# Layer 1 of a linear-attention and MLP kernel: a row of ones in the key weights, and the keys' feature map in one VectorE operation

## The chip, the cores and the metric

The kernel runs on one core of one Trainium2 chip. The metric is the device time of one execution in microseconds (us). The kernel before was run three times: 760.4, 760.68 and 760.71 us, median 760.68 us. One further execution was recorded by the hardware profiler; its span, from the first to the last instruction, is 758.4 us.

The engines are called as the profile calls them: PE (TensorE matmuls), PEld (TensorE weight loads), DVE (VectorE), ACT (ScalarE), POOL (GpSimd), SP (SyncE, which issues the transfers here).

## The reference, cut to what matters

A linear attention block A and an MLP block B alternate twice over 2048 tokens of width 576. Everything below concerns the feature map `phi` of the first block A.

```python
def _A_ref(x, wqkv, wo):                       # x: (1, 2048, 576), already layer-normed
    H = 32; Dh = D // H                        # 32 heads of 18
    q, k, v = split(x @ wqkv)
    phi = lambda t: jnp.where(t > 0, t + 1, jnp.exp(t)) + 1e-6
    pq, pk = phi(q), phi(k)
    kv = jnp.einsum("bhsd,bhse->bhde", pk, v)
    z = jnp.einsum("bhsd->bhd", pk)
    num = jnp.einsum("bhqd,bhde->bhqe", pq, kv)
    den = jnp.einsum("bhqd,bhd->bhq", pq, z)[..., None] + 1e-6
    return (num / den).reshape(B, S, D) @ wo

x = x + _A_ref(_layernorm(x), A_wqkv, A_wo)    # layer 1: li = 0 in the kernel
x = x + _B_ref(_layernorm(x), ...)             # li = 1
x = x + _A_ref(_layernorm(x), A_wqkv, A_wo)    # li = 2
x = x + _B_ref(_layernorm(x), ...)             # li = 3
```

## The kernel before, in words

The 2048 tokens are 16 row tiles of 128 (`NT`). For PE the normed rows are also needed turned: `yT` holds them as five chunks of 128 features (576 is 4.5 chunks, and the lower half of chunk 4 meets zero weights). In layer 1 a row tile is loaded (L188), its mean and variance are taken on DVE (L397, L398, L404), it is normed in place (L444 on POOL, L449 on DVE for tiles 0 to 3), PE transposes its five blocks (L500, out `tp`) and ACT copies them into `yT` (L505; tiles 0 and 1 are split between ACT L502 and DVE L503). Normed columns 512 to 575 do not stay in the row: a second norm instruction writes them to `v_ring`, beside a column of ones put there at the start (L222, L223). These 65 columns are called the tail.

The attention never forms V per token. For each half of the 576 key columns (288, `HALF`) and each row tile, `k_half` (L650) makes the keys in PSUM, `phi` turns them into `pk`, and `rows_by_keys` (L668) adds normed rows times `pk` into four accumulators (`acc`, 128 rows each) and a fifth for the tail (65 rows, the 65th being the sum of `pk` over tokens, `z`). In the loop over row tiles only half 0 is summed. Half 1 is kept and summed after the loop (`last_rows_by_keys`, `sums`).

Two forms of `phi` stand in layer 1 before the change:

- half 0 (`phi_from_psum`, L547; tile 2 excepted): ACT exp (L554), ACT adds 1 + 1e-6 (L555), then DVE takes min and adds 1e-6 (L560) and takes the max of two bf16 tiles in SBUF (L562). PSUM is last read by ACT.
- half 1 (`phi_by_dve`, L535): ACT exp (L537), DVE min and add (L539), DVE adds to the PSUM operand and takes the max (L541). PSUM is last read by DVE.

PSUM has eight banks. Four belong to the two pairs `accA` and `accB`; four (`ps_h`, L41) go round among everything else. From the start of the tail sums to the end of the loop the tail's accumulator (L673) holds one of these four, so keys of half 0 (`k_ps`), keys of half 1 (`k_ps`), the transposes (`tp`) and one query product (`q_ps`, L621) of each row tile go round in three.

The order of PE is the program's order, since every matmul is chained to the one before (`pe`, L166). In the loop of layer 1 (L860 to L868, t = 4 to 15) it is, for each t: keys half 0, keys half 1 (5 matmuls each), five transposes of a later row tile, one query product (5 matmuls of 512 columns), then the sums of row tile t (the tail first, then four). The queues of the other engines are ordered by the tile framework, except where the program adds an order: the beginning is written out by hand for DVE and ACT in two lists (`in_order`, L854 to L856; names such as `n0` norm, `nt0` norm of the tail, `s0a` statistics, `e00` exp, `id00` add, `mi00` min, `ma00` max, tile and half), later statistics stand behind the last max of the keys, and `yT` copies stand behind the last exp of the keys. The queue of SP is chained for the loads.

In layer 3 (li = 2) the normed rows come back through DRAM: `load_row` loads columns 0 to 511 (L293) and a separate transfer per four row tiles loads the tails (L333). One query product per row tile stands there too, but no transposes: rows are turned by DVE and transfers.

Of the kernel before, what the change touches and what calls it, by code (L numbers as in the profile page):

```python
# [15 lines left out]
P = 128  # L16
# [14 lines left out]
HALF = D // 2  # L31
LAST_PARTS = (slice(0, 3 * P), slice(3 * P, D))
# [3 lines left out]
def build(tc, A_x, A_wqkv, A_wo, B_w1, B_b1, B_w2, B_b2, out, dbg=None, n_layers=4):  # L36
    nc = tc.nc
    dbg = dbg or {}
    with ExitStack() as ctx:
# [95 lines left out]
        NV = 2  # L135
        v_ring = [const.tile([P, G, P], BF16, name=f"v_ring{i}") for i in range(NV)]
# [10 lines left out]
        def row_tile(name):  # L147
            return rows.tile([P, D], F32, name=name, tag="row")

        x0_tiles = {}  # L150

# [32 lines left out]
        def load_x0(t):  # L184
            if t % 2 == 0:
                x0_tiles["pair"] = rows.tile([P, 2, D], BF16, name="x0", tag="row")
            x0 = x0_tiles["pair"][:, t % 2, :]
            chained(nc.sync.dma_start(out=x0, in_=x_in[t * P:(t + 1) * P, :]))  # L188
            x0_tiles[t] = x0
# [31 lines left out]
        for vr in v_ring:  # L221
            nc.gpsimd.memset(vr[:], 0.0)  # L222
            nc.gpsimd.memset(vr[:].rearrange("p g c -> p (g c)")[:, 0:520].rearrange("p (t e) -> p t e", e=65)[:, :, 64:65], 1.0)  # L223
# [42 lines left out]
        def tail_of(t):  # L266

            flat = v_ring[t // 8][:].rearrange("p g c -> p (g c)")
            return flat[:, (t % 8) * 65:(t % 8 + 1) * 65]

        def tails(c):
            flat = v_ring[c // 2][:].rearrange("p g c -> p (g c)")
            return flat[:, (c % 2) * 260:(c % 2 + 1) * 260].rearrange("p (t e) -> p t e", e=65)

        def first_tail(t, width=65):

            slot = 2 * (t % 8) + t // 8
            flat = v_ring[slot // 8][:].rearrange("p g c -> p (g c)")
            return flat[:, (slot % 8) * 65:(slot % 8) * 65 + width]

# [8 lines left out]
        def load_row(t):  # L289
            if t % 2 == 0:  # L290
                pair = rows.tile([P, 2, D], BF16, name="yrow_pair", tag="row")
                row_of[t], row_of[t + 1] = pair[:, 0, :], pair[:, 1, :]
            load = nc.sync.dma_start(out=row_of[t][:, 0:4 * P], in_=yrow_d[t // TPC, t % TPC].rearrange("j r d -> (j r) d")[:, 0:4 * P])  # L293
            if t >= 6:
                behind(load, "landed")
# [20 lines left out]
        def land(now=False):  # L316

            for it in list(landing):
                it[0] -= 1
                if it[0] > 0 and not now:  # L320
                    continue
                _, home, c, kind = it
                landing.remove(it)
                cols = slice(c * CB, (c + 1) * CB)
                nc.sync.dma_start(out=yT[:, 0:KD - 1, cols],
                                  in_=home[0:16, :, :].rearrange("(k jj) r n -> (jj r) k n", jj=4))
                for hi in range(2 if kind == "B" else 1):
                    landed = nc.sync.dma_start(out=yT[64 * hi:64 * (hi + 1), KD - 1, cols],
                                      in_=home[16:18, :, :].rearrange("jj r n -> (jj r) n"))
                if kind == "A":  # L330
                    if c == NCB - 1:
                        sp_last["landed"] = landed.ins.name
                    tail = nc.sync.dma_start(out=tails(c)[:, :, 0:64],  # L333
                                             in_=yrow_d[c].rearrange("i j r d -> (j r) i d")[:, :, 4 * P:D])
                    behind(tail, "landed")
                    if c == NCB - 1:
                        for t in range(c * TPC, NT):
                            load_row(t)
# [8 lines left out]
        class LNPipe:  # L347
# [11 lines left out]
            def tick(self, transposes=1):  # L359
                land()  # L360
                for it in list(self.items):
# [77 lines left out]
                    elif st in (2, 3) and it["kind"] == "A" and it["evac"] == "act":  # L439
                        xt, t = it["xt"], it["t"]  # L440
                        tail = first_tail(t)[:, 0:64]
                        if it["norm"] == "pool":
                            for out, cols in ((xt[:, 0:4 * P], slice(0, 4 * P)), (tail, slice(4 * P, D))):
                                norm = nc.gpsimd.tensor_scalar(out=out, in0=xt[:, cols], scalar1=it["rstd"][:, 0:1],  # L444
                                                               scalar2=it["nmr"][:, 0:1], op0=ALU.mult, op1=ALU.add)
                            pool_last["norm"] = norm.ins.name
                        else:
                            for name, out, cols in ((f"n{t}", xt[:, 0:4 * P], slice(0, 4 * P)), (f"nt{t}", tail, slice(4 * P, D))):
                                norm = named(name, nc.vector.tensor_scalar(  # L449
                                    out=out, in0=xt[:, cols], scalar1=it["mv"][:, 0:1], scalar2=it["rstd"][:, 0:1],  # L450
                                    op0=ALU.subtract, op1=ALU.mult))
                            dve_last["norm"] = norm.ins.name
# [30 lines left out]
                    elif st == 4:  # L483
# [14 lines left out]
                        for k in range(KD):  # L498
                            block = first_tail(t, P) if first_layer and k == 4 else y[:, k * P:(k + 1) * P]
                            pe(nc.tensor.transpose(out=(tp if k < 3 else tp2)[:, k, :], in_=block, identity=ident[:]))  # L500
# [34 lines left out]
        def phi_by_dve(ps_ap, out_ap, rows, n, tag=None):  # L535
            e = exp_tile(tag)
            exp = nc.scalar.activation(out=e[0:rows, 0:n], in_=ps_ap, func=ACT.Exp)  # L537
            act_last["exp"] = exp.ins.name
            low = nc.vector.tensor_scalar(out=e[0:rows, 0:n], in0=e[0:rows, 0:n], scalar1=1.0, scalar2=1e-6,  # L539
                                          op0=ALU.min, op1=ALU.add)  # L540
            top = nc.vector.scalar_tensor_tensor(out=out_ap, in0=ps_ap, scalar=C1, in1=e[0:rows, 0:n],  # L541
                                                 op0=ALU.add, op1=ALU.max)
            dve_last["phi"] = top.ins.name
            if tag is not None:
                named("e" + tag, exp), named("mi" + tag, low), named("ma" + tag, top)

# [68 lines left out]
        def layer_A(li, next_kind, pre_a1=None):  # L615
# [34 lines left out]
            def k_half(t, half, defer=False):  # L650
# [5 lines left out]
                by_dve = half or li == 0 and t == 2  # L656

                def phi():
                    if (half, t // 2) not in self_k["pk"]:
                        self_k["pk"][(half, t // 2)] = blk.tile([P, D], BF16, name="pk", tag="blk")  # L660
                    pk = self_k["pk"][(half, t // 2)][:, (t % 2) * HALF:(t % 2 + 1) * HALF]
                    (phi_by_dve if by_dve else phi_from_psum)(kp[:, 0:HALF], pk, P, HALF,
                                                              tag=f"{t}{half}" if li == 0 and t < 4 else None)
                if defer:
                    return phi
                phi()

            def rows_by_keys(t, half, chunks=(4, 0, 1, 2, 3), done=True):  # L668
# [5 lines left out]
                pk = self_k["pk"][(half, t // 2)][:, (t % 2) * HALF:(t % 2 + 1) * HALF]  # L674
                for k in chunks:
                    dst = self_k["tail"][0:65, 0:HALF] if k == 4 else self_k["acc"][k // 2][:, k % 2, 0:HALF]
                    lhsT = (tail_of(t) if li > 0 else first_tail(t)) if k == 4 else row_of[t][:, k * P:(k + 1) * P]
                    pe(nc.tensor.matmul(dst, lhsT=lhsT, rhs=pk, start=(t == 0), stop=(t == NT - 1)))  # L678
                cols = slice(half * HALF, (half + 1) * HALF)
                if 4 in chunks and t == NT - 1:  # L680
                    nc.gpsimd.memset(zk[:, cols], 0.0)
                    nc.scalar.copy(out=k2[4][0:64, cols], in_=self_k["tail"][0:64, 0:HALF])
                    nc.scalar.copy(out=zk[64:65, cols], in_=self_k["tail"][64:65, 0:HALF])
                if not done:
                    return
                if t % 2:
# [7 lines left out]
                for i, copy in enumerate((nc.scalar.copy, nc.vector.tensor_copy)):  # L694
                    for j in range(2):
                        copy(out=k2[2 * i + j][:, cols], in_=self_k["acc"][i][:, j, 0:HALF])

            def last_rows_by_keys():

                parts = [ps_h.tile([P, 512], F32, name=name, tag="h") for name in ("z_rows", "k2_tail")]  # L700
                for size, part in zip((32, 64), parts):
                    n = P // size
                    for t in range(NT):
                        tail = tail_of(t) if li > 0 else first_tail(t)
                        lhsT = tail[:, 64:65].to_broadcast([P, 32]) if size == 32 else tail[:, 0:64]
# [3 lines left out]
                nc.scalar.activation(out=zk[:, HALF:D], in_=parts[0][:, 0:HALF], func=ACT.Identity, scale=1.0 / 32)  # L709
                nc.scalar.copy(out=k2[4][:, HALF:D], in_=parts[1][:, 0:HALF])  # L710
# [36 lines left out]
            def z_stage():  # L747
                zp = ps_h.tile([P, 512], F32, name="z_ps", tag="h")
                for g in range(G):
                    pe(nc.tensor.matmul(zp[0:GR[g], g:g + 1], lhsT=zk[:, GO[g]:GO[g] + GR[g]],  # L750
                                        rhs=(tail_of(0) if li > 0 else first_tail(0))[:, 64:65],
# [73 lines left out]
            if li == 0:  # L825
# [3 lines left out]

                def feed_and_tick(t, n):  # L830
                    feed0(t, after=dve_last["phi"] if t > 5 else None)
                    for _ in range(n):
# [21 lines left out]
                in_order("s0a s0b g0 s1a s1b n0 nt0 g1 cd0 n1 nt1 s2a s2b g2 cd1 mi00 s3a n2 nt2 s3b ma00 g3 u3 mi10 s4a "  # L854
                         "mi11 n3 ma10 nt3 ma11 mi20 ma20 mi21 s4b ma21 g4 u4 mi01 ma01 s5a s5b mi30 g5 mi31 u5 ma30 ma31")
                in_order("ln0 re0 ln1 re1 ca0 e00 ca1 ln2 re2 id00 e01 e10 ca2 e11 id10 e20 e21 ca3 e31 e30 id30 ca4")  # L856
# [292 lines left out]
        for li, kind in enumerate(kinds):  # L1149
# [11 lines left out]
            else:  # L1161
                pe_chain.update(on=True)
# [50 lines left out]
```

## Time and profile before

| | before |
|---|---|
| runs, us | 760.4, 760.68, 760.71 |
| median, us | 760.68 |
| profiled execution, span, us | 758.4 |
| PE busy | 753.2 us, 99% |
| ACT busy | 328.7 us, 43% |
| DVE busy | 272.0 us, 36% |
| POOL busy | 116.6 us, 15% |
| granted TensorE clock | 1.000 |
| layer 1 to its first MLP matmul | 0 to 101.8 us |

The profiled execution is told by its span; the 2.3 us between the span and the median of the runs lie around it. A timeline line reads: start, length, engine, line, operation, output <- input, size; in brackets the idle time of the engine just before and what ended it. The chain of work that ended last reads: start, length, engine and what it ran; it names at each moment the one piece of work that the end waited for. A group line reads: line, engine, operation, names, shapes, count | busy us, mean ns | idle before.

### The profile page before, as it was taken

The numbers are of one execution on the slowest core, as the hardware profiler recorded it, in microseconds if no ns is written. First come the engines' busy times: TensorE is split into PE (matmuls) and PEld (weight loads), VectorE is DVE, ScalarE is ACT, GpSimd is POOL, SyncE is SP. The second block draws the span as 40 slices with busy tenths as digits, with TensorE's granted clock in tenths as the row PEclk, the third lists the DMA queues.
The fourth block names the chain that finished last, engine by engine and source line by source line (L and its number), as shares of the span: only waits on it lengthen the run. The fifth ranks groups of instructions, "written<-read, shape, count | busy, mean of one in ns | idle before, by whom it ended". The sixth has DMA issues, their size and how long they took to land.

```text
span 758.4 us, 15817 instructions
## 1 busy us (share of the span) xinstructions
PE 753.2 (99%) x6595; PEld 487.4 (64%) x6595; DVE 272.0 (36%) x685; ACT 328.7 (43%) x733; POOL 116.6 (15%) x196
## 2 busy tenths in 40 slices
PE   9999999999999999999999999999999999999998
PEld 5776754774477457646777777457646754774476
DVE  8876862136033503401367577600230131000000
ACT  6887656205600650263057666660174036205600
POOL 4840231002000301200100005300020020001000
PEclk9999999999999999999999999999999999999999
DMA  8994573026312711320404047530240033011000
GB/s 236 267 313 74 178 262 82 17 64 189 83 39 83 181 51 48 109 69 17 131 24 116 24 136 255 185 82 16 88 115 7 16 127 82 9 33 55 1 9 24
DMA packets 80977, 73.90 MB, mean 97 GB/s; under 512 B 36874, under 2 KB 65546, under 8 KB 80906
## 3 DMA queue, kind: packets, MB, share of 16 engines
q1 hardware_dynamic: 80906, 72.90, 33.0%
q8 instruction: 51, 0.84, 0.5%
q14 instruction: 20, 0.16, 0.1%
HBM read 48.10 MB, written 24.77 MB: 96 GB/s over the span
## 4 chain that ended last, share of the span: by engine, by line
PE 97%; DVE 1%; ACT 0%; issue 0%; DVEq 0%
PE m_ps L1104 36%; PE h_ps L1045 21%; PE hp_ps L1045 16%; PE q_ps L621 6%; PE k_ps L653 5%; PE wo_ps L933 5%; PE k_ps L678 4%; PE m_half L1104 1%; PE tp L500 1%; PE warm_ps L217 1%; PE k_tail L678 1%; PE kv_ps L719 0%; PE den_ps L769 0%; PE rden_ps L810 0%; PE kvwo_half L737 0%
## 5 line engine op out<-in xcount | busy, mean ns | idle before, releaser
L1104 PE MATMUL m_ps<-w_sb,hT 128*128 128x288 bf16 x2232 | 274.8, 286 | 0.0
L1104 PEld LDWEIGHTS <-hT 128*128 128x128 bf16 x2304 | 224.3, 98 | 60.4 <-issue 3.4
L1045 PEld LDWEIGHTS <-w_sb 64*128 64x128 bf16 x2304 | 124.5, 94 | 136.4 <-issue 1.9
L1045 PE MATMUL hp_ps<-yT,w_sb 64*128 64x512 bf16 x1152 | 178.0, 376 | 0.0
L1045 PE MATMUL h_ps<-yT,w_sb 64*128 64x512 bf16 x1152 | 148.0, 376 | 0.0
L1050 ACT COPY relay_sb<-relay_sb 128x1 f32<-128x1 f32 x144 | 28.5, 198 | 260.4 <-PE h_ps L1045 217.6
L1041 ACT ACTIVATE hT<-h_ps,b1T 128x512 bf16<-128x512 f32 x144 | 91.0, 683 | 44.1 <-PE h_ps L1045 44.1
L433 POOL TENSOR_TENSOR ln_rstd<-ln_u,neg_half 128x1 f32<-128x1 f32 x61 | 35.2, 577 | 439.9 <-DVE ln_u L415 218.0
L1041 ACT ACTIVATE hT<-hp_ps,b1T 128x512 bf16<-128x512 f32 x144 | 91.1, 692 | 0.0
L605 DVE TENSOR_TENSOR xbf<-m_ps,xo 128x576 bf16<-128x576 f32 x15 | 11.4, 757 | 213.5 <-PE m_ps L1104 213.5
L605 DVE TENSOR_TENSOR xo<-m_ps,xo 128x576 f32<-128x576 f32 x16 | 12.1, 757 | 172.6 <-PE m_ps L1104 172.6
L588 POOL TENSOR_TENSOR xo<-xo,b_bc 128x576 f32<-128x576 f32 x32 | 40.9, 1283 | 97.3 <-DMA xo<-x_d 58.4
L1045 PE MATMUL h_ps<-yT,w_tail 64*128 64x512 bf16 x144 | 54.1, 376 | 0.0
L1045 PE MATMUL hp_ps<-yT,w_tail 64*128 64x512 bf16 x144 | 54.1, 376 | 0.0
L621 PE MATMUL q_ps<-yT,wqkv_sb 128*126 128x512 bf16 (+1 forms) x200 | 49.3, 379 | 0.1
L653 PE MATMUL k_ps<-wqkv_sb,yT 128*128 128x288 bf16 x320 | 44.6, 286 | 0.2
L933 PE MATMUL wo_ps<-kvwo,pq 126*128 126x288 bf16 (+1 forms) x320 | 43.4, 286 | 0.3
L1045 PEld LDWEIGHTS <-w_tail 64*128 64x128 bf16 x288 | 27.1, 94 | 17.1
L653 PEld LDWEIGHTS <-yT 128*128 128x128 bf16 x320 | 31.0, 98 | 8.9 <-ACT yT L502 0.6
L933 PEld LDWEIGHTS <-pq 126*128 126x128 bf16 (+1 forms) x320 | 30.3, 97 | 9.1 <-issue 0.8
L621 PEld LDWEIGHTS <-wqkv_sb 128*126 128x126 bf16 (+1 forms) x200 | 25.7, 131 | 11.7 <-issue 0.5
L554 ACT ACTIVATE phi_e<-q_ps 126x512 bf16<-126x512 f32 (+1 forms) x40 | 23.9, 597 | 18.4 <-PE q_ps L621 16.8
(138 smaller groups left out, 591.6 us busy)
## 6 DMA issues: line engine op xcount, KB each, us to landing
xo<-x_d SPq DMA_DIRECT2D x48, 288.0 KB, 3.5
x_d<-xo SPq DMA_DIRECT2D x32, 288.0 KB, 2.6
xl<-x_d SPq DMA_DIRECT2D x24, 288.0 KB, 4.2
y_d<-turned SPq DMA_DIRECT2D x40, 144.0 KB, 3.1
w_sb<-in_B_w_dram SPq DMA_DIRECT2D x6, 864.0 KB, 10.4
yT<-y_d SPq DMA_DIRECT2D x10, 512.0 KB, 4.2
w_sb<-in_B_w_dram SPq DMA_DIRECT2D x9, 512.0 KB, 5.9
x_d<-xn SPq DMA_DIRECT2D x16, 288.0 KB, 3.3
```

The costliest lines, as they stand in the source:

```text
L433: nc.gpsimd.tensor_tensor(out=rstd[:], in0=it["u"][:], in1=neg_half[:], op=ALU.pow)
L554: exp = nc.scalar.activation(out=e_out, in_=ps_ap, func=ACT.Exp)
L588: nc.gpsimd.tensor_tensor(out=xo[:], in0=xo[:], in1=b2_bc[:], op=ALU.add)
L605: total = nc.vector.tensor_tensor(out=xn[:, cols].rearrange("p (h n) -> p h n", h=2), in0=halves, in1=xo[:, cols].rearrange("p (h n) -> p ...
L621: pe(nc.tensor.matmul(qp[0:GR[g], :], lhsT=wqkv_sb[:, k, GO[g]:GO[g] + GR[g]], rhs=yT[:, k, c * CA:(c + 1) * CA], start=(k == 0), stop=(k ...
L653: pe(nc.tensor.matmul(kp[:, 0:HALF], lhsT=yT[:, k, t * P:(t + 1) * P], rhs=wqkv_sb[:, k, D + half * HALF: D + (half + 1) * HALF], start=(k ...
L678: pe(nc.tensor.matmul(dst, lhsT=lhsT, rhs=pk, start=(t == 0), stop=(t == NT - 1)))
L933: pe(nc.tensor.matmul(wp[:, half, 0:HALF], lhsT=pq[(g, c)][0:GR[g], j * P:(j + 1) * P], rhs=kvwo[g][0:GR[g], half * HALF:(half + 1) * HALF ...
L1041: act_last["gelu"] = nc.scalar.activation(out=to, in_=ps, func=ACT.Gelu_apprx_tanh, bias=b1T[:, f:f + 1], scale=1.0).ins.name
L1045: mm = pe(nc.tensor.matmul(dst[n], lhsT=wt, rhs=mv, start=(seen[n] == 0), stop=(seen[n] == 8)))
L1050: relay = nc.scalar.copy(out=relay_sb[:, 1:2], in_=relay_sb[:, 0:1])
L1104: pe(nc.tensor.matmul(acc[half][:, 0:cols.stop - cols.start], lhsT=hT[f][:, j * P:(j + 1) * P], rhs=w2_sb[:, f, cols], start=(f == 0), sto ...
```

## The change

In layer 1 only, the keys' feature map is rewritten. Row 64 of chunk 4 of the key weights is set to one (it was zero), and the normed rows get ones behind column 575, so that the product in PSUM is x + 1. Then `phi` is one ACT exp with bias -1 and one DVE operation, min(max(x + 1, 1), exp(x)), for both halves. The 1e-6 is left out there and added to the sums: key sums of half 0 get a further column of ones in `pk` (289 columns), which makes the row sums; 1e-6 times these is added where the accumulators are copied out.

Row tiles are 640 wide, with ones in columns 576 to 639; so the norm is one instruction for all 576 columns, the tail is read from the row itself, and `v_ring` is gone. In layer 3 the ones are written by a POOL memset for each pair of rows, the row loads have 576 columns, and the separate tail loads are gone. POOL sets the weights' row of ones back to zero in layer 2.

```diff
+        nc.vector.memset(wqkv_sb[64:65, 4, D:2 * D], 1.0)
+        nc.gpsimd.memset(neg_one[:], -1.0)
+        nc.gpsimd.memset(key_eps[:], 0.0)
+        nc.gpsimd.memset(key_eps[:, 6:7], 1e-6 * S / P)
+        for pair in x0_pairs:
+            nc.gpsimd.memset(pair[:, :, D:RW], 1.0)
...
-            load = nc.sync.dma_start(out=row_of[t][:, 0:4 * P], in_=yrow_d[...][:, 0:4 * P])
+                nc.gpsimd.memset(pair[:, :, D:RW], 1.0)
+            load = nc.sync.dma_start(out=row_of[t][:, 0:D], in_=yrow_d[...])
...
-                            for out, cols in ((xt[:, 0:4 * P], slice(0, 4 * P)), (tail, slice(4 * P, D))):
-                                norm = nc.gpsimd.tensor_scalar(out=out, in0=xt[:, cols], ...)
+                            norm = nc.gpsimd.tensor_scalar(out=xt[:, 0:D], in0=xt[:, 0:D], ...)
...
+        def phi_of_first(ps_ap, out_ap, n, tag=None):
+            e = exp_tile(tag)[:, 0:n]
+            exp = nc.scalar.activation(out=e, in_=ps_ap, func=ACT.Exp, bias=neg_one[:, 0:1])
+            act_last["exp"] = exp.ins.name
+            top = nc.vector.scalar_tensor_tensor(out=out_ap, in0=ps_ap, scalar=1.0, in1=e, op0=ALU.max, op1=ALU.min)
+            dve_last["phi"] = top.ins.name
...
+                    if li == 0 and half == 0:
+                        pk = self_k["pk"][(0, t)] = blk.tile([P, D], BF16, name="pk", tag="blk")
+                        nc.gpsimd.memset(pk[:, HALF:HALF + 1], 1.0)
+                        phi_of_first(kp[:, 0:HALF], pk[:, 0:HALF], HALF, tag=f"{t}0" if t < 4 else None)
+                        return
...
+                    if li == 0:
+                        phi_of_first(kp[:, 0:HALF], pk, HALF, tag=f"{t}1" if t < 4 else None)
...
+                if summed and t == NT - 1:
+                    for i in range(2):
+                        nc.vector.tensor_scalar(out=key_eps[:, 2 * i:2 * i + 2].unsqueeze(2),
+                                                in0=self_k["acc"][i][:, :, HALF:HALF + 1], scalar1=1e-6, ...)
+                    for rows_, col in ((slice(0, 64), 4), (slice(64, 65), 5)):
+                        nc.vector.tensor_scalar(out=key_eps[rows_, col:col + 1],
+                                                in0=self_k["tail"][rows_, HALF:HALF + 1], scalar1=1e-6, ...)
...
-                in_order("s0a s0b g0 s1a s1b n0 nt0 g1 cd0 n1 nt1 s2a s2b g2 cd1 mi00 s3a n2 nt2 s3b ma00 g3 u3 mi10 s4a "
-                         "mi11 n3 ma10 nt3 ma11 mi20 ma20 mi21 s4b ma21 g4 u4 mi01 ma01 s5a s5b mi30 g5 mi31 u5 ma30 ma31")
-                in_order("ln0 re0 ln1 re1 ca0 e00 ca1 ln2 re2 id00 e01 e10 ca2 e11 id10 e20 e21 ca3 e31 e30 id30 ca4")
+                in_order("s0a s0b g0 s1a s1b n0 g1 cd0 n1 s2a s2b g2 cd1 s3a ma00 n2 s3b g3 u3 ma10 s4a "
+                         "n3 ma11 ma20 s4b ma21 g4 u4 ma01 s5a s5b g5 u5 ma30 ma31")
+                in_order("ln0 re0 ln1 re1 ca0 e00 ca1 ln2 re2 e01 e10 ca2 e11 e20 e21 ca3 e31 e30 ca4")
...
+                if li == 1:
+                    nc.gpsimd.memset(wqkv_sb[64:P, 4, D:2 * D], 0.0)
```

## The prediction, on record before the result

> **What bounds the kernel now.** I read the page first: busy shares, then the chain that ended last.
>
> ```profile
> span 758.4 us, 15817 instructions
> ...
> PE 753.2 (99%) x6595; PEld 487.4 (64%) x6595; DVE 272.0 (36%) x685; ACT 328.7 (43%) x733; POOL 116.6 (15%) x196
> ...
> PE 97%; DVE 1%; ACT 0%; issue 0%; DVEq 0%
> ```
>
> PE sets the end almost alone, and the change takes no matmul away. So time can be won only where the chain is not PE, and lost wherever PE is made to wait. The chain in order of time, for layer 1, shows both places:
>
> ```profile
> 1.31 4.02 PE warm_ps L217 x9
> ...
> 11.08 0.30 DVE pk L562
> 11.38 0.21 DVE v_ring L449
> 11.60 0.37 DVE pk L541
> ...
> 12.01 0.44 PE tp L500 x5
> ...
> 29.09 0.28 PE tp L500 x5
> 29.37 1.15 PE q_ps L621 x5
> ...
> 55.28 1.08 PE q_ps L621 x5
> ```
>
> From 5.99 to 11.97 us the chain is DVE's queue; afterwards PE runs from piece to piece. Third, one round of the loop from the timeline (start, length, engine):
>
> ```profile
> 31.04 1.39 PE L653 MATMUL k_ps<-wqkv_sb,yT 128*128 128x288 bf16 x10
> ...
> 31.85 0.41 ACT L554 ACTIVATE phi_e<-k_ps 128x288 bf16<-128x288 f32 x1 [0.21 <-PE k_ps L653]
> ...
> 32.16 0.41 ACT L555 ACTIVATE phi_a<-k_ps 128x288 bf16<-128x288 f32 x1
> ...
> 32.48 0.22 PE L500 MATMUL tp<-ident,v_ring 128*128 128x128 bf16 x1
> ...
> 32.61 1.24 PE L621 MATMUL q_ps<-yT,wqkv_sb 128*126 128x512 bf16 x5
> ...
> 32.77 0.69 ACT L505 COPY yT<-tp 128x640 bf16<-128x640 bf16 x1
> ...
> 33.41 0.46 DVE L541 SCALAR_TENSOR_TENSOR pk<-k_ps,phi_e 128x288 bf16<-128x288 f32 x1
> ```
>
> See who gives `q_ps` its bank. Three banks go round here. Keys half 0, keys half 1 and `tp` hold them when the query product wants one; half 0's is free first, once ACT's addition (L555) has read it: 32.16 + 0.41 = 32.57, and the query product starts at 32.61. There is no slack at all: it takes 1.15 us in the chain where transposes stand before it and 1.08 at t = 15 without them. The 0.07 may also be the weight load behind transposes; either way the bank comes just in time.
>
> **The beginning.** The hand-written DVE list loses four `nt` (a tail norm starts 0.20 us before the next instruction) and all `mi` (0.14 to 0.20 of the chain each). I ran the new lists forward with the old spacings (norm of 576 columns 0.34, statistics 0.37, max from PSUM 0.37, ACT 0.31 between two keys' passes). One start cannot move, because it is a weight transfer:
>
> ```profile
> 7.61 1.09 PEld L653 LDWEIGHTS <-yT 128*128 128x128 bf16 x10 [0.20 <-DMA wqkv_sb<-in_A_wqkv_dram]
> ```
>
> Step by step, new start with the old in brackets. Keys of tile 0: 6.37 (6.51), since the sum of tile 1's statistics no longer stands behind a tail norm. Their exp ends at 7.61 (7.75); ACT then copies tile 1 (7.50), takes Ln (7.86) and exp (8.20 to 8.40) for the rstd of tile 2. DVE meanwhile: statistics of tile 3 at 7.7 (8.08), first max 8.05, norm of tile 2 at 8.43 (8.58, now held by rstd). PE turns tile 2 and starts half 1 of tile 1 at 9.21 (9.34), tile 2's keys at 10.31 (10.44). DVE: statistics 8.77, their sum 9.25, variance 9.49, POOL's power 9.72 to 10.28, max of tile 1 half 0 at 9.56, statistics 9.93, norm of tile 3 at 10.32 (10.76), max of half 1 10.66 to 11.11 (11.51 to 11.96). That max frees a bank for the transposes of tile 3, now before PE wants it: they start when PE is through, 11.56 (12.01). Tile 2's max ends at 12.01, ahead of its sums at 12.34, and tile 3's keys start at 12.84 against 13.27. **Gain 0.43.** Bounds: PE's own work from 7.61 to there is 25 key matmuls of 0.123, 12 sums of 0.122 and two times five transposes in 0.28, together 5.1, so it can't be through before 12.72 and the gain is at most 0.55; it is zero if a row still in flight holds the statistics of tile 3. The added DVE memset of 576 bf16 columns costs nothing up to 0.1: DVE waits 0.46 us for the first row (first statistics at 3.06), and 512 such columns take 0.48. POOL's start loses two 0.63 us memsets of `v_ring` and gets eight narrow ones; a narrow one (128 x 8) is 0.13.
>
> **The loop.** For half 0 the last reader of PSUM is now DVE's one operation. It can't start before exp has ended, where the old addition on ACT overlapped exp. Its price is the old L541, the same operation on the same shapes:
>
> ```profile
> L541 DVE SCALAR_TENSOR_TENSOR pk<-k_ps,phi_e 128x288 bf16<-128x288 f32 x11 | 5.0, 458 | 0.4
> ...
> L562 DVE TENSOR_TENSOR pk<-phi_a,phi_e 128x288 bf16<-128x288 bf16 x11 | 3.6, 328 | 1.2
> ...
> L560 DVE TENSOR_SCALAR phi_e<-phi_e 128x288 bf16<-128x288 bf16 x11 | 2.6, 233 | 0.8
> ```
>
> Exp can't come earlier: it waits for PE (the last key matmul of the half starts 4 x 0.123 after 31.04 and lasts 0.286, so 31.82). Exp ends at 32.26; ACT to DVE takes 0.03 (the max of a query product starts at 54.59 after an ACT end at 54.56); 0.46; DVE to PE 0.05 (11.60 is the chain's share; the record of that L541 ends at 11.96, PE goes on at 12.01). So the query product starts at 32.80 instead of 32.61: **0.19 us lost per round**. Rounds with transposes ahead of a query product are t = 4 to 14, eleven in the chain: 11 x 0.19 = **2.1 us**. Nothing hides it, since PE's queue is in order and the sums and all later matmuls stand behind the query product. At t = 15 `tp` is missing and its bank is free.
>
> This is a lower end if DVE comes late. In the old round DVE was late: busy 2.92 of 3.27 us (mean of six rounds in the stretches view), and min and max of half 0 ran 0.7 us after exp. Now it loses 0.24 (L539, mean 240 ns) + 0.23 and changes 0.33 for 0.46, so 2.58 of 3.46, and its order for a round (two keys' max, statistics, query's min and max) puts the query's max before half 0's: that ends at ACT's end of the previous query product, 0.66 after the round's start, + 0.03 + 0.43 = 1.12, ahead of 1.25. So I take 0.19 and keep 0.37 more (one statistics instruction in front) for the range. A memset of `pq` (L629, 0.48) stands on DVE twice in these rounds, at 28.99 just ahead of half 0's min: 0 to 0.5 each; I take **0.2** for both, since DVE has 0.9 idle per round to fit it.
>
> The Trainium skill, in "VectorE: DVE Perf Modes", section on the trn2 errata, gives a VectorE operation from PSUM 120 + elements cycles at 0.96 GHz; for 288 that is an estimate of 0.425 us. The row says 0.458. By the page the loop would lose 1.75 us and the sum below would be 0.35 smaller; the row is used.
>
> **The rest.** 289 instead of 288 columns in 80 sums: from 288 to 512 columns spacing goes from 0.123 to 0.213, 0.4 ns a column, 0.03 us in all; the far end is the spacing of 512, 80 x 0.09 = 7.2. I take 0.03, the nearer row. The end of the loop: four small DVE operations on PSUM (a 72 x 32 one is 0.18) come before ACT's copies of the tail (57.36), whose bank the next sums want at 59.06; the copies end at 58.16, so up to 0.9 later costs nothing on that bank, and ACT's copy for the `z` product has some 0.5: 0 to 0.3, I take **0.1**. In layer 3 each row load grows from 1024 to 1152 bytes a row and four loads of 128-byte pieces go; the chain there is PE alone, and POOL, 15% busy, sets the ones: 0. The memset of the weights' ones in layer 2 falls where POOL is idle: 0. ACT loses twelve additions of 0.41; it already waited for PE: 0.
>
> **Sum:** -0.43 + 2.1 + 0.2 + 0.03 + 0.1 = +2.0. The profiled execution (758.4) would come to 760.4; 2.3 us lie around it, so on the median of the runs: **762.7 us**. About 0.2% (1.5 us) is what a measurement of this kernel can tell from no change: below 759.2 faster, above 762.2 slower.
>
> **The rivals.**
> - *Only the beginning counts* (0.27): the query product finds its bank without waiting, because the framework hands banks round otherwise than I read it. Then 760.68 - 0.43 + 0.1 = **760.4**, not slower. For it: PE waits for nothing else in the waits view, and the 0.07 can be the weight load. Against: three banks, three holders, and no fourth. It decides if half 0's max ends before 32.57 in that round's terms.
> - *DVE comes late* (0.12): one statistics instruction (0.37) stands before half 0's max in each round: 11 x 0.37 = 4.1 more, **766.8**. For: DVE's order is not written out in the loop. Against: its slack.
> - *The bank handed over is that of `tp`* (0.05): free when the copy ends, at 32.74 + 0.69 = 33.43; with the 0.04 from ACT to PE (32.57 to 32.61) that is 0.86 late, 11 x 0.86 = 9.5, and with the beginning and the rest **769.9**.
> - *289 columns are dear* (0.04): toward 7 us more, **767 to 770**.
> - *POOL's memset of the ones in `pk` is late* (0.04): behind a norm that ends 1 us after the sums were due, up to **772**.
>
> The forecast has 0.48, its own range 761.6 to 764.0 (0.10 to 0.35 per round). The range 760.1 to 766.0 takes in the first rival, the forecast and half of the second: about 0.8. Faster by over 0.2%: 0.02, since the beginning can't give 1.5 us. Within: the first rival and the forecast's lower quarter, 0.39. Slower: 0.59.
>
> **What would show it.** Right: in the chain `q_ps` x5 near 1.33 in rounds t = 4 to 14, with a DVE piece on `pk` between `tp` and `q_ps`, DVE's idle time there going up, and `tp` of tile 3 at about 11.5. Wrong: `q_ps` at 1.15 (first rival); a DVE max that starts more than 0.1 after its exp (second); sums spaced wider than 0.125 (fourth); a wait of the tail's sums on POOL (fifth).

## The result and the profile after

The changed kernel takes 773.26 us (median of four runs, 772.28 to 773.91); the kernel before took 760.54 us in four runs beside it (760.40 to 760.71). The ratio is 1.0166, with a 95% interval of 1.0154 to 1.0178: 12.7 us slower. The forecast was 762.7 us, with a range up to 766.0. The direction was right and the size was not.

The profiled execution after has a span of 772.0 us, 13.6 more than before's 758.4. From the page of the kernel after:

```profile
span 772.0 us, 15770 instructions
...
PE 756.0 (98%) x6595; PEld 488.1 (63%) x6595; DVE 269.5 (35%) x654; ACT 329.4 (43%) x718; POOL 115.2 (15%) x216
...
PE 89%; DMA 5%; SPq 3%; POOL 1%; ACT 1%; issue 0%; DVE 0%; POOLq 0%
```

PE is busy for 2.8 us more although it runs the same 6595 matmuls, and its share of the chain falls from 97% to 89%: transfers, SP's queue and POOL now stand in it. These eight points are not the time lost: followed back from the stop, the chain runs through the transfers to the start, and PE's work of the first 64 us drops out of it. The chain of the kernel after, in order of time, shows where:

```profile
50.91 13.00 DMA b_raw<-in_B_b_dram
63.91 0.06 issue
63.97 0.21 POOL b1T L261
64.18 0.08 POOL pk L655 x2
64.26 0.01 issue
64.27 0.40 PE k_tail L691
...
65.64 2.40 PE k_ps L649 x10
68.04 1.72 PE q_ps L617 x5
```

Read it backwards from `k_tail`. The tail sums of tile 14 waited for a POOL memset on `pk` (L655). That memset is the one that the change added: it sets the 289th column of `pk`, the ones. It waited for a cast (L261) that turns the MLP's bias into f32, and the cast waited for the load of that bias, issued at 50.91 us and landed 13.00 us later. The bias is needed by nobody here; its cast only stands ahead in POOL's queue. The same cast is in the kernel before, at nearly the same time, and there POOL's next work was not urgent (timeline of the kernel before):

```profile
63.84 0.21 POOL L254 CAST b1T<-b_raw 128x36 f32<-128x36 bf16 x1 [12.76 <-DMA b_raw<-in_B_b_dram]
```

The waits view of the kernel after (what PE waited for: total us, times, longest) has two new rows at its head:

```profile
PE k_tail L691 <- POOL pk L655: 7.1, 1, 7.1
PE q_ps L617 <- DVE pk L538: 2.7, 11, 0.6
```

The stop has a sequel. The stretches view of the kernel after around it, with the columns stretch, us, busy us (and count) of PE, PEld, DVE, ACT and POOL, then the granted clock, DMA share and GB/s:

```profile
57.00:64.20 7.20, 0.16 (x1) 0.00 (x0) 0.72 (x2) 1.09 (x2) 0.23 (x3) 0.64 0.72 68
64.20:66.00 1.80, 1.73 (x8) 1.10 (x8) 0.00 (x0) 0.00 (x0) 0.05 (x2) 0.50 0.00 0
66.00:68.00 2.00, 2.00 (x10) 1.37 (x9) 0.46 (x1) 0.50 (x1) 0.00 (x0) 0.50 0.00 0
68.00:70.00 2.00, 2.00 (x10) 1.15 (x9) 0.54 (x2) 0.71 (x2) 0.57 (x1) 0.70 0.00 0
```

When PE resumes at 64.2, the granted clock is 0.50, and it is back at 1.00 only after about 69.2 (the mean of 0.70 from 68 to 70 is 0.50 for 1.2 us and 1.00 for the rest). It fell during the stop: the mean of 0.64 from 57.00 to 64.20 is 1.00 for 2.0 us and 0.50 for the rest, so it fell at 59.0, some 1.9 us after PE stopped at 57.16. The ten key matmuls take 2.40 us of the chain there instead of ten times 0.123, and the query product 1.72 instead of 1.08.

Last, a round of the loop, in the timeline of the kernel after:

```profile
32.77 1.39 PE L649 MATMUL k_ps<-wqkv_sb,yT 128*128 128x288 bf16 x10
...
33.58 1.11 ACT L536 ACTIVATE phi_e<-k_ps,neg_one 128x288 bf16<-128x288 f32 x2
...
34.11 0.46 DVE L538 SCALAR_TENSOR_TENSOR pk<-k_ps,phi_e 128x288 bf16<-128x288 f32 x1 [0.22 <-ACT phi_e L536]
...
34.62 1.24 PE L617 MATMUL q_ps<-yT,wqkv_sb 128*126 128x512 bf16 x5 [0.19 <-DVE pk L538]
```

From the keys to the query product it is 34.62 - 32.77 = 1.85 us, where it was 32.61 - 31.04 = 1.57 before. The query product waits for DVE's one operation on half 0, as forecast, but 0.09 longer than forecast: exp ends later.

**Where the 13.6 us are.** Points that both traces have, as offsets of after against before: keys of tile 4, 17.92 against 17.91: nothing won or lost by then. Tail sums of tile 14: due at 57.16 (64.27 less the wait of 7.11) against 53.27, though in an execution without the wait they start at 57.00 (first experiment), so 3.7 lost in the loop. They start at 64.27: 7.3 for the wait. The first query product behind the loop, 70.21 against 56.80, is 13.4 late, so 2.4 more went in the stretch of low clock. First MLP matmul, 115.16 against 101.74: still 13.4. The remaining 0.2 are spread over 650 us.

### The profile page after: what moved, and what is told of

The parts are those of the page before. It is cut to its first block, busy times and chain, and to the rows that moved or that the text cites. A ratio compares the mean times of both kernels' runs of the same rounds, so it can differ in the third digit from the quotient of the medians.

```text
span 772.0 us, 15770 instructions
## 1 busy us (share of the span) xinstructions
PE 756.0 (98%) x6595; PEld 488.1 (63%) x6595; DVE 269.5 (35%) x654; ACT 329.4 (43%) x718; POOL 115.2 (15%) x216
## 4 chain that ended last, share of the span: by engine, by line
PE 89%; DMA 5%; SPq 3%; POOL 1%; ACT 1%; issue 0%; DVE 0%; POOLq 0%
PE m_ps L1129 36%; PE h_ps L1070 20%; PE hp_ps L1070 16%; PE wo_ps L958 4%; PE q_ps L617 4%; PE k_ps L691 3%; PE k_ps L649 3%; DMA w_sb<-in_B_w_dram 2%; DMA b_raw<-in_B_b_dram 2%; DMA wqkv_sb<-in_A_wqkv_dram 2%; SPq L246 1%; PE m_half L1129 1%; SPq L241 1%; SPq L190 1%; PE kv_ps L743 0%
```

## The experiments

The theory after the result: three things cost time, each by itself. POOL's memset behind the bias cast stops PE once; the low clock after it is a consequence of the stop and not of anything else in the change; and each round of the loop loses 0.28, of which 0.19 is the bank and 0.09 a longer exp. The main rivals: the stop would move to another wait when POOL is freed (the landing of the bias would be what matters, or DVE); the low clock is brought by the new instructions; the rounds are longer for another reason, such as the 289th column or DVE's order.

The first four ran beside twelve runs of the kernel before (median 760.37 us), the other four beside 27 more (760.15 us).

### 1. The cast behind the ones

The cast of the bias is ordered behind the last memset of ones on POOL. Nothing else differs from the kernel after.

```diff
+            tc.add_manual_dep(cast.ins, pool_last["ones"], NOSYNC, reason="ones of the keys first")
...
-                        nc.gpsimd.memset(pk[:, HALF:HALF + 1], 1.0)
+                        pool_last["ones"] = nc.gpsimd.memset(pk[:, HALF:HALF + 1], 1.0).ins.name
```

> The changed kernel with one order added on POOL: the cast of the MLP's bias stands behind the last memset of ones of the keys. Theory (four causes: 3.7 us of longer rounds in the loop, 7.1 us in which PE waits for a POOL memset that is queued behind the cast, 2.4 us of work at a lower granted clock after that pause, nothing from the beginning): 773.3 - 7.1 - 2.4 = 763.7 us, clock 1.0 throughout, no wait of the tail's sums on POOL. Rival A, the low clock has another cause (the 289-column sums, say): about 766, granted clock still near 0.77 from 60 to 80 us. Rival B, the memsets come late for another reason: 773 as before.

Measured: 764.21 us (764.20 to 764.24), ratio 1.0050 (1.0034 to 1.0067), clock 1.000. One line of order takes back 9.05 of the 12.7 us. In the waits view of this kernel POOL's row is gone and DVE's row is what it was:

```profile
PE q_ps L618 <- DVE pk L539: 2.7, 11, 0.6
```

So the stop was POOL's queue: the landing of the bias itself holds nobody. Between the profiled executions (762.3 against 772.0) it is 9.7, the 7.3 of the wait and the 2.4 of the clock.

### 2. A pause alone, in the kernel before

To see whether a pause brings the low clock without anything of the change, the kernel before gets 15 POOL memsets of a tile that is not in use at that time, and then rewrites the column of ones of tile 14's tail, which the tail sums wait for.

```diff
+                    if t == 14:
+                        behind_it = pool_last["norm"]
+                        for out in [y_ring[2][:]] * 15 + [first_tail(t)[:, 64:65]]:
+                            ones = nc.gpsimd.memset(out, 1.0)
+                            tc.add_manual_dep(ones.ins, behind_it, NOSYNC, reason="one after the other")
+                            behind_it = ones.ins.name
+                        pool_last["norm"] = behind_it
```

> The kernel before with nothing of the change, but a pause: ahead of the tail sums of row tile 14, POOL writes a scratch tile fifteen times (0.62 us each) and then the column of ones that these sums read, so that PE stops for some 7 us at the place where it stopped in the changed kernel. Theory (a pause costs its length and then work at about half the granted clock): 7.1 + 2.4, 770 us, granted clock near 0.5 for some 5 us behind the pause. Rival, a pause costs its length alone and the low clock belongs to the change: 767.6, clock 1.0 right behind it.

Measured: 770.70 us (769.97 to 771.33), ratio 1.0135 (1.0120 to 1.0150). The profiled one (769.97) in the waits view and the stretches view:

```profile
PE k_tail L678 <- POOL v_ring L871: 8.0, 1, 8.0
```

```profile
53.50:60.20 6.70, 0.00 (x0) 0.00 (x0) 1.04 (x3) 1.06 (x2) 6.13 (x11) 0.80 1.19 280
60.20:64.00 3.80, 2.55 (x11) 1.63 (x12) 0.00 (x0) 0.00 (x0) 1.14 (x3) 0.50 0.64 76
64.00:66.00 2.00, 2.00 (x13) 1.31 (x12) 1.15 (x4) 1.13 (x4) 0.21 (x1) 0.91 0.02 4
```

The clock falls to 0.50 here too, and the profiled execution takes 9.6 us more than the kernel before for a pause of 8.0. So the low clock follows the stop and needs no new instruction. Here it fell later: the mean of 0.80 from 53.50 to 60.20 is 1.00 until 57.5, some 4.1 us after PE stopped at 53.44. The pause came out longer than meant, and the 1.6 us that the clock cost beyond it are less than the 2.4 in the kernel after: the total expected was about right, its two parts were not.

### 3. ACT reads the bank last

On top of experiment 1: for half 0 of t = 4 to 15, ACT copies the keys to SBUF behind its exp, and DVE reads the copy. The bank is then free when ACT is through, as in the kernel before.

```diff
+            if copied:
+                a = work.tile([P, 512], BF16, name="phi_a", bufs=2)[:, 0:n]
+                nc.scalar.copy(out=a, in_=ps_ap)
+                ps_ap = a
```

> As e1, and in the loop (t from 4) ACT copies half 0's keys from PSUM to SBUF behind the exp, and DVE's one operation reads the copy: ACT is again the last reader of the bank, as before the change. Theory (the query product waits for half 0's bank): rounds go back from 3.55 to 3.27 to 3.35 us, since the copy overlaps exp; 11 x 0.2 to 0.28 and the two rounds with a memset ahead, 760.2 to 761.2. Rival, the rounds are longer because DVE or exp is slower, whoever reads last: 763 or more, as e1 or worse, as ACT has 0.4 us more per round.

Measured: 762.40 us (762.30 to 762.86), ratio 1.0027 (1.0016 to 1.0037), 1.8 less than experiment 1. A round is 3.345 us instead of 3.55, and DVE's row is gone from the waits view. The timeline of this kernel in one round:

```profile
33.10 0.39 ACT L541 CAST phi_a<-k_ps 128x288 bf16<-128x288 f32 x1
...
33.54 1.24 PE L622 MATMUL q_ps<-yT,wqkv_sb 128*126 128x512 bf16 x5
```

The copy ends at 33.49 and the query product starts at 33.54. So it is half 0's bank that the query product waits for, and its last reader frees it. It is 1.66 us behind the keys (31.88) where it was 1.57 before: the missing 0.09 pointed at exp, which ends later. Two new waits of 0.4 us (on POOL's `head_bc` and on DVE's `ln_st`, both ahead of tail sums) stand in the way too. From the keys of tile 4 to those of tile 15 it is 37.85 us, 39.70 in experiment 1 and 35.98 before: of the 3.7 us of the loop 1.8 are won and 1.9 remain, for exp and in the two rounds with these waits. The expectation had counted neither, and the time lies above its 760.2 to 761.2.

### 4. The bias in the instruction

On top of experiment 1: the -1 of exp is a number in the instruction instead of a column in SBUF.

```diff
-            exp = nc.scalar.activation(out=e, in_=ps_ap, func=ACT.Exp, bias=neg_one[:, 0:1])
+            exp = nc.scalar.activation(out=e, in_=ps_ap, func=ACT.Exp, bias=-1.0)
```

> As e1, but exp's bias of -1 is a number in the instruction instead of a tile. Theory (0.09 of each round's 0.28 is exp, 0.50 us with a tile as bias against 0.41 without): exp takes 0.41 again, 11 x 0.09 = 1.0 us less in the loop and 0.1 to 0.4 less in the beginning: 762.3 to 762.6. Rival, the longer exp has another cause (the range of its argument): 763.7 as e1, exp still 0.50.

Measured: 763.15 us (763.14 to 763.30), ratio 1.0037 (1.0024 to 1.0050), 1.06 less than experiment 1. The groups view, first of the kernel after, then of this one:

```profile
L536 ACT ACTIVATE phi_e<-k_ps,neg_one 128x288 bf16<-128x288 f32 x27 | 13.5, 501 | 12.8 <-PE k_ps L649 10.2
```

```profile
L537 ACT ACTIVATE phi_e<-k_ps 128x288 bf16<-128x288 f32 x27 | 11.1, 411 | 5.1 <-PE k_ps L650 3.8
```

Exp takes 0.41 us again. A round is 3.46 us against 3.265 before: 0.195, close to the 0.19 of the forecast. The beginning gains as well: tile 3's keys start at 13.04 and tile 4's at 17.68, 0.23 earlier than before. The two rounds with longer waits (t = 4 and t = 7) do not get shorter: 3.75 and 4.0 us here and in experiment 1. The time lies above the 762.3 to 762.6 expected, which had counted eleven rounds and 763.7 for experiment 1.

### 5. Both

Experiments 3 and 4 together.

> Both edits together: ACT copies half 0's keys (from t = 4), and exp's bias is a number in the instruction. Theory: the copy ends 0.70 us after exp's start, as the old addition did (0.72), so the rounds go back to 3.27 from 3.35, and the beginning gains the 0.23 seen with the number: 762.4 - 11 x 0.08 - 0.2 = 761.3, with the two single stalls of 0.4 left. Rival, the two edits share one gain: 762.3.

Measured: 761.07 us (761.00 to 761.49), ratio 1.0012 (1.0003 to 1.0022). Most rounds are 3.26, as before. What is left over the kernel before, 0.9 us, is in single waits, the rest not told apart from these:

```profile
PE k_tail L696 <- POOL pk L660: 0.7, 2, 0.3
```

In both, the ones in `pk` stand behind a norm on POOL, as the fifth rival of the prediction has it (a norm ends at 20.90, the ones at 20.96, the tail sums start at 21.00).

### 6. Cover instead of a copy

Instead of freeing the bank sooner, PE is given other work meanwhile: on top of experiment 4, the sums of row tile t - 1 stand between the keys of t and the transposes. ACT's copy of experiment 3 is not in it.

```diff
+                    if t > 4:
+                        rows_by_keys(t - 1, 0)
...
-                    rows_by_keys(t, 0)
+                rows_by_keys(NT - 1, 0)
```

> DVE's one operation stays the last reader of half 0's bank (bias in the instruction, cast behind the ones), but PE does the sums of the row tile before (0.61 us) between the keys and the transposes, so that the query product asks for the bank 0.6 us later. Theory (a wait for the bank of 0.19 per round, hidden by any 0.2 us of work in between): the waits of the query product vanish, 11 x 0.19 and most of two single waits of 0.4 to 0.55: 763.15 - 2.1 - 0.8 = 760.3, rounds of 3.27. Rival A, the wait moves to the next holder in the ring (transposes wait for the query product's bank): 761 to 763. Rival B, DVE or ACT are late in any order: 763.

Measured: 760.53 us (760.37 to 760.82), ratio 1.0005 (0.9996 to 1.0014): not to be told from the kernel before. DVE's row in its waits view shrinks from 2.7 us in 11 waits to one:

```profile
PE q_ps L618 <- DVE pk L539: 0.4, 1, 0.4
```

Rounds are mostly 3.24. Everything of the change is in this kernel but the column for the bias, the order on POOL and the order on PE. It is 0.31 us behind the kernel before at the first query product behind the loop (57.11 against 56.80), 0.32 at the first MLP matmul (102.06 against 101.74) and 0.2 at the end (758.6 against 758.4), so the end of layer 1 and layer 3 cost nothing that these traces show. Nor does the 289th column: four sums take 0.49 us of the chain in both kernels.

### 7. POOL sets the weights' row

On top of experiment 6, to look for the rest of the beginning: the memset of the row of ones, 0.54 us on DVE ahead of the first statistics, goes to POOL.

```diff
-        nc.vector.memset(wqkv_sb[64:65, 4, D:2 * D], 1.0)
+        nc.gpsimd.memset(wqkv_sb[64:65, 4, D:2 * D], 1.0)
```

> As e6, and the row of ones in the weights is set by POOL instead of DVE. In the changed kernel that DVE memset made the first statistics start at 3.34 instead of 3.06. Theory: 0.28 comes back at the first transposes, and less further on, since a weight transfer holds PE until 7.5: 0.1 to 0.25 under e6. Rival, the weight transfer hides all of it: as e6.

Measured: 760.58 us (760.33 to 760.86), ratio 1.0005 (0.9996 to 1.0014): nothing. The first statistics do start at 3.02 instead of 3.34 and the first transposes at 5.24 instead of 5.55, but the keys of tile 0 start at 6.60 all the same, and their five matmuls take 1.09 us instead of 0.79. PE itself was slow there: the two warm-up matmuls ahead of the keys (512 columns) take 0.63 us each, as query products did at a granted clock of 0.50 behind the stop, and 0.38 in experiment 6, though the clock's column reads 1.00 in both. So in this execution the slow start of PE lasted into the keys and used up the 0.3 us. Whether it did in the other ten, and why, stays open.

The trace of experiment 6 shows a second holder. Tile 3's keys start at 13.20 there, as in experiment 5, 0.07 earlier than before and not 0.23 as in experiment 4. Its chain:

```profile
4.44 3.64 DMA x<-in_A_x_dram
...
8.10 0.04 DVE ln_st L388
...
8.48 0.44 DVE pk L539
8.92 0.35 DVE x L437
```

A row still in flight holds the statistics of tile 3 until 8.10 (7.93 in experiment 4), and tile 2's norm, which its transposes wait for, stands behind them in DVE's order.

### 8. A shorter pause

Experiment 2 with eight memsets instead of 15, to see how long a pause has to be.

> The kernel before with a pause half as long (eight scratch memsets of 0.69 us instead of fifteen): PE stops for about 3.4 us at row tile 14 instead of 8.0. Theory (the granted clock falls only some 2 to 4 us into a pause): length alone or with little more, 763.8 to 764.5, clock about 1.0 behind it. Rival, any pause of PE halves the clock behind it: 3.4 + 1.4 to 2.4, 765.2 to 766.2.

Measured: 764.89 us (763.46 to 766.27), ratio 1.0062 (1.0048 to 1.0076). The profiled execution (763.46) waited 3.2 us with a granted clock of 1.00 throughout, and cost 3.3 us, the pause alone. The other three had a mean clock of 0.996 to 0.997 and took 1.4 to 2.8 us longer; how long PE waited in them is not on record. So with this pause the low clock comes in some executions and not in others: neither expectation holds for all of them.

## Why the prediction was wrong, step by step

- **The step that failed** is the price of the ones in `pk`, a POOL memset of 0.10 us for each row tile: the sum has no term for it. ("POOL, 15% busy, sets the ones: 0" is said of layer 3, and there it held.) Only the fifth rival prices it, "behind a norm that ends 1 us after the sums were due", up to 772 with a chance of 0.04, outside the range. What stood ahead of the memset was a cast that does nothing for 10.58 us but wait for a transfer. Before's own trace shows that cast with 12.76 us of idle time, at 63.84. A count of POOL's work hides it, since a waiting engine counts as idle. The price was 7.3 us (experiment 1). The rival named the right wait and the right memset, and the wrong thing ahead of it; that its 772 lies near the measured time is luck. What it described, ones behind a norm, came to 0.7 us in two waits of experiment 5.
- **A term that was not in the sum** is the clock. The forecast priced every wait at its length. This one cost 2.4 us more, because PE came back at half the clock (experiments 1 and 2).
- **The loop's mechanism was right.** Half 0's bank, freed by DVE instead of ACT, costs 0.19 per round: experiment 4 measures 3.46 against 3.265. Freed by ACT again (3 and 5), or covered by other work (6), it is gone. The first rival, that the query product finds its bank free, is refuted by the waits view and by these.
- **Mis-sized: exp.** "Exp ends at 32.26" took 0.41 from the old exp without a bias. With the column of -1 it takes 0.50. Without it, experiment 4 takes back 0.09 in each of nine rounds and 0.23 in the beginning, 1.06 us in all. The loop's 3.7 us, for which the forecast had 2.1 and 0.2, are 0.28 in each of nine rounds, 2.6, and 1.1 in the rounds t = 4 and t = 7.
- **The memsets of `pq`:** 0.2 was taken. The one at 30.05 us stands just ahead of half 0's operation and makes the wait 0.64 instead of 0.19 (t = 7); the other, at 50.27, makes no wait longer. In t = 4 it is 0.39, because statistics and a query's max are still ahead on DVE, a piece of the second rival in one round, not in eleven.
- **The beginning:** 0.43 was forecast, 0 came. In the kernel after, tile 2's norm starts at 8.81 and not at 8.43: ACT, whose exp is longer, is through with its rstd only at 8.78. With the bias in the instruction the gain was 0.23 in one trace (experiment 4) and 0.07 in two (5 and 6), where the condition came true that the prediction itself had named for a gain of zero: a row in flight holds the statistics of tile 3. The weights' row of ones, "nothing up to 0.1" on DVE, made the first statistics 0.28 late; experiment 7 could not show what that costs, so the other 0.2 has no shown cause.
- **The rest:** 289 columns, the end of the loop and layer 3 were put at 0.13 together; experiment 6 leaves 0.4 us in all, and its trace none of it behind the loop. The fourth rival falls. The rival by `tp` (0.86 per round) falls with experiment 3.
- **Right direction, wrong range:** the loop alone would have given 764.2 (experiment 1), which the range held. The stop and its clock put the time 7 us past its end.

No version here beats the kernel before. The change takes work off DVE and ACT, which the chain hardly passes through after the beginning, and what it won there is under 0.3 us.

## What to carry to other kernels

When an instruction is added to an in-order queue, even a small memset on an engine that is 15% busy, read what stands ahead of it in that queue, and look at the idle time before that work and what ended it: a cast that waits 12 us for a transfer is a wall for everything behind it. When an engine's operation becomes the last reader of a PSUM bank, the price is its end less the old reader's end, per round; and before speeding it up, see whether PE has other work to put in between, which here made the price vanish. Count a stop of the matmul engine of several microseconds at more than its length.

## What the runs showed of the hardware

- After a wait of 7.1 us PE ran some 5 us at a granted clock of 0.50, after one of 8.0 us some 3; after one of 3.2 us the clock stayed at 1.00 in one execution, and three others of that kernel, by their mean clock of 0.996 to 0.997, had a low stretch. It fell some 1.9 us into the stop of 7.1 us and some 4.1 us into that of 8.0. The Trainium skill, in "TensorE: Matmul & The Clock Gate", part 1 on the HAM clock gate, says that the clock halves after an idle window of about 3.4 us that runs free of the kernel, and comes back after as long a busy one. The traces agree on the half, and on stretches that differ from one execution to the next; the 3 and 5 us lie on both sides of the page's figure. A fall after 1.9 us is earlier than a whole idle window of that length allows: there the trace differs from the page, and the trace decides.
- Exp on 128 x 288 from PSUM takes 0.50 us with its bias from a column in SBUF and 0.41 with a number in the instruction. The Trainium skill, in "ScalarE: Activation LUTs", section "What ACT_TABLE_LOAD costs", gives about 93 ns for each such column; the measured difference is 501 - 411 = 90 ns.
- DVE's max and min in one operation on 128 x 288 took 0.47 us in experiment 3's round with both operands in SBUF as bf16 (start 33.52), and 0.46 with one of them in PSUM: copying the operand to SBUF did not make it faster. A plain max of two bf16 tiles of that size took 0.33 in the kernel before.
